# Chunks 0 and 1 of the first mixture: plain float32 out projection, and chunk 1's attention in a fixed order

## The chip, the cores and the metric

The kernel runs on one core of one Trainium2 chip. The metric is the device time of one execution in microseconds; the profile's span, from the first to the last instruction, is shown beside it. Engines are named TensorE (PE in the rows, its weight loads PEld), VectorE (DVE), ScalarE (ACT), GpSimd (POOL) and SyncE (SP, which issues nearly all DMAs here).

## The reference

Three layers follow one another. All arrays are float32; two batches, 8 heads, 768 positions, head width 40, so 1536 tokens of width 320; 1536 hidden columns.

```python
# attention (an mLSTM), for each position t
m_new = max(f_gate + m, i_gate)
C = exp(f_gate + m - m_new) * C + exp(i_gate - m_new) * outer(v, k)
n = exp(f_gate + m - m_new) * n + exp(i_gate - m_new) * k
y[t] = sigmoid(o_gate) * (C @ q) / max(abs(n . q), 1)
# first layer, on all tokens
x = (sigmoid(x @ w_gate) * (x @ w_val)) @ w_out
# second layer, with its own weights
xn = x / sqrt(mean(x * x) + 1e-6) * rms_g
g = xn @ w_gate
out = (g * sigmoid(g) * (xn @ w_val)) @ w_out
```

## The kernel before, in words

**Tiles and steps.** The positions are cut into 6 chunks of 128; a chunk holds both batches, so 256 tokens (`T`), of which batch `b` is one half. The hidden columns are cut into 12 blocks `f` of 128. The first layer is a list of 72 steps (chunk, block): `moe` (line 741) makes 16 gate and value matmuls of 256 columns (line 747) into a PSUM bank `g`; ScalarE takes the sigmoid (749), VectorE the product with the value half (750). `moe_out` (776) multiplies the result `h` with the out weights and accumulates both halves over all 12 blocks in two PSUM banks `o`. The second layer has 36 steps over pairs of chunks (`moe2`, `moe2_out`).

**Split operands.** TensorE works in a reduced float32 format (F32R). An operand is held as a high part and a low part, the difference to the original, and a product is three matmuls. For `h` ScalarE copies the high part (752) and GpSimd subtracts (753, by `sub`, line 194); `moe_out` then has three matmuls a half, six a step (785). Weights are prepared block by block: `load_w` brings a block as packed 64-bit words (960 KB); `conv_w` (138) with `conv_1` and `conv_2` turns the words into float32, two passes on ScalarE (161, 172) and two on VectorE (184, 191); `split_w` (202) makes high parts (copies by ScalarE, 198) and low parts (194, GpSimd or VectorE by the tables `G1`, `O1`) of the gate, value and out weights.

**Attention.** The part of a chunk for one batch: scores (`a_s`, line 357, plain float32), their product with the decay (`a_p`, 366), the inter part from the carried state (`a_inter`, 403 and 405), the weighted sum (`a_pv`, 426), the state update (`a_u`, 435 to 444), and an end (`a_h`, 455 to 464; `a_h0` for chunk 0) that finishes `x`; `a_x` transposes `x` and splits it into `xT` (522 and 194), which the steps of that chunk read.

**Order.** `ORDER` lists the chunk of each of the first 24 steps. Everything else hangs on step numbers: `at(t, ...)` puts a piece of attention, a load or a conversion of weights ahead of step t, and the loop at line 827 issues the events of a step, the step, and the out matmuls of the step `SKEW` = 2 before. A scheduler then chooses the order on each engine; the code up to line 715 (chunk 0's attention, blocks 0 and 1) is pinned by `pin` (716) in the order in which it is written, and what follows is issued behind it.

```python
ORDER = '000000111100001100111111'
C1S = (-4, -2)
```

Of the kernel before, what the change touches and what calls it, by code (L numbers as in the profile page):

```python
# [30 lines left out]
SKEW = 2  # L31
WARM = 5
# [7 lines left out]
ORDER = '000000111100001100111111'  # L40
# [8 lines left out]
PINNED = ('EngineType.PE', 'EngineType.DVE', 'EngineType.Activation', 'EngineType.Pool')  # L49
# [17 lines left out]
def mlstm_moe_kernel(ctx, tc, gate_if, gate_s, qk, qg, tok, w1, w2, rms_g, cst, out):  # L67
# [55 lines left out]
    def load_tok(c, b):  # L123
        t = tok_t[c, b] = p2.tile([128, 8 * 122], F32, tag="tok", name="tok").rearrange("p (h e) -> p h e", h=8)
        nc.sync.dma_start(out=t, in_=tok[c, b])
        if c:
            g = qg_t[c, b] = p1.tile([120, 3, L], F32, tag="qg", name="qg")
            nc.sync.dma_start(out=g, in_=qg[c, b])

    wg_t, wo_t, wraw, wc, conv = {}, {}, {}, {}, {}  # L130

# [69 lines left out]

    def split_w(f, go=0, oo=0, both=True, eng=None):
# [3 lines left out]
        w = wo_t[f] = wp.tile([128, 2, DM], F32R, tag=f"wo{f}", name="wo")  # L206
        eng = eng or nc.scalar
        copy(eng, t[:, :, 0:2, :], g)
        copy(eng, t[0:64, 0, 2, :], r[0:64])
        copy(eng, t[64:128, 1, 2, :], r[64:128])  # L210
        copy(eng, w[:, 0, :], o)

        def low():
            sub(nc.vector, t[64:128, 0, 2, :], r[0:64], t[0:64, 0, 2, :])
            sub(nc.gpsimd, t[0:64, 1, 2, :], r[64:128], t[64:128, 1, 2, :])

        if go:
# [314 lines left out]
    def a_x(c, b):  # L532
# [65 lines left out]
    at(16, lambda: nc.gpsimd.tensor_scalar(out=rmsg, in0=rmsg, scalar1=2.0 ** -16, scalar2=None, op0=ALU.mult))  # L598
# [41 lines left out]
    load_w(w1, 1)  # L640
    p = nc.gpsimd
# [21 lines left out]
    a_p(0, 1)  # L663
    gates_r2()
# [61 lines left out]
    after = ExitStack()  # L726
    for k in pin(first).values():
        after.enter_context(tc.issue_after(k))
    nc.sync.dma_start(out=selg, in_=cst[0:U, CW:CW + 120])
    nc.sync.dma_start(out=selc, in_=cst[0:U, CW + 120:])  # L730
    nc.sync.dma_start(out=rmsg, in_=rms_g)
    gates_r5()
# [4 lines left out]
    load_qk(1, 0)  # L737
    load_tok(1, 0)


    def moe(c, f):
# [7 lines left out]
        nc.scalar.activation(out=sg, in_=g[:, 0, :], func=AF.Sigmoid, scale=2.0 ** -8)  # L749
        nc.vector.tensor_tensor(out=sg, in0=sg, in1=g[:, 1, :], op=ALU.mult)  # L750
# [25 lines left out]
    def moe_out(c, f):  # L776
        h = hst.pop((1, c, f))
        w = wo_t_used[1, f]
        for b in range(B):
# [3 lines left out]
            n = slice(b * L, (b + 1) * L)  # L783
            for i, (hs, ws) in enumerate(((0, 0), (0, 1), (1, 0))):
# [42 lines left out]
    for i in range(min(ev), len(seq) + SKEW):  # L827
# [10 lines left out]
        while 0 <= i and done < len(seq) and done <= i - (SKEW if seq[done][0] == 1 else 1):  # L838
# [87 lines left out]
```

## Time and profile before

| | us |
|---|---|
| median of 3 runs (518.36 to 520.56) | 518.44 |
| the profiled execution | 518.81 |
| its span | 517.0 |
| TensorE busy | 490.7 |
| VectorE busy | 306.6 |
| GpSimd busy | 238.5 |
| ScalarE busy | 228.9 |

The mean granted TensorE clock over the span is 0.969 of full speed. Busy time is the union of an engine's instructions. Matmuls are pipelined, so a busy TensorE is not one at its peak; what a matmul costs in a row of equal ones is read from start to start. A plain float32 matmul stands in the trace as two records, a reduced one as one. In a row, `out<-in` are the program's names, `xN` is a count, and the idle time behind a row names what ended it.

### The profile page before, as it was taken

To read this page: it belongs to the slowest core of one execution; us is meant where nothing else is said; L and a number is where in the kernel's file an instruction comes from. 1 tells how busy PE (TensorE), PEld (TensorE's weight loads), DVE (VectorE), ACT (ScalarE), POOL (GpSimd) and SP (SyncE) were. 2 spreads that over 40 slices of the span, in tenths; PEclk is the share of its full clock that TensorE was granted. 3 is DMA by queue.
4 is the path that set the end of the run, shared out by engine and by line. 5 is a ranking of instruction groups with operands and counts; after the bars stand their busy time and mean duration, and the time that the engine had idled before them with its cause. 6 is when DMAs were issued, how large, how long until landed. Compare 5 with 4: busy or idle time off the path is not lost.

```text
span 517.0 us, 8591 instructions
## 1 busy us (share of the span) xinstructions
PE 490.7 (95%) x3324; PEld 445.8 (86%) x3324; DVE 306.6 (59%) x551; ACT 228.9 (44%) x507; POOL 238.5 (46%) x267
## 2 busy tenths in 40 slices
PE   8896958999999999999999978999999999999997
PEld 5676847999999999999999867888888888888886
DVE  6869989853285785967878996723243223432223
ACT  3655757523354443445468756522243222431222
POOL 2758884653355545644337995621212221122220
PEclk9977966999999999999999999999999999999999
DMA  7667656220031140302354323100010000100001
GB/s 243 185 231 234 226 196 222 90 81 30 12 121 37 44 150 11 81 16 77 112 199 166 136 77 105 48 0 2 0 53 0 1 0 2 45 7 1 0 1 51
DMA packets 12558, 42.60 MB, mean 82 GB/s; under 512 B 1590, under 2 KB 4870, under 8 KB 12518
## 3 DMA queue, kind: packets, MB, share of 16 engines
q1 hardware_dynamic: 12278, 41.84, 24.3%
q8 instruction: 26, 0.43, 0.3%
q10 hardware_dynamic: 240, 0.22, 0.2%
q14 instruction: 14, 0.11, 0.1%
HBM read 40.05 MB, written 2.00 MB: 81 GB/s over the span
## 4 chain that ended last, share of the span: by engine, by line
PE 72%; DVE 12%; POOL 5%; DMA 4%; ACT 4%; issue 3%; POOLq 0%; ACTq 0%; SPq 0%
PE g L747 13%; PE g L761 13%; PE a L761 13%; PE o L810 12%; PE o L785 8%; DMA wraw<-in_w_dram 4%; PE o L747 3%; DVE wg L194 2%; DVE wc L184 2%; POOL wg L194 2%; DVE wc L191 1%; POOL wo L194 1%; PE a L357 1%; ACT wg L198 1%; POOL h L194 1%
## 5 line engine op out<-in xcount | busy, mean ns | idle before, releaser
L747 PE MATMUL g<-xT,wg 128*128 128x256 f32 x912 | 130.6, 295 | 1.8 <-DVE sig L750 1.3
L747 PEld LDWEIGHTS g<-xT,wg 128*128 128x128 f32 x912 | 121.2, 200 | 4.1 <-DVE sig L750 1.5
L194 POOL TENSOR_TENSOR ft<-p,fb 128x512 fp32r<-128x512 f32 x35 | 45.2, 1292 | 131.0 <-ACT fb L770 131.0
L194 POOL TENSOR_TENSOR h<-sig,h 128x256 fp32r<-128x256 f32 x72 | 64.7, 900 | 77.3 <-ACT h L752 76.3
L785 PE MATMUL o<-wo,h 128*128 128x320 f32 x432 | 79.7, 317 | 12.2 <-POOL h L194 10.4
L764 DVE TENSOR_TENSOR p<-p,g 128x512 f32<-128x512 f32 x36 | 24.5, 687 | 92.1 <-ACT p L763 92.1
L785 PEld LDWEIGHTS o<-wo,h 128*128 128x128 f32 x432 | 65.9, 192 | 15.2 <-POOL h L194 12.5
L810 PE MATMUL o<-wo,fb 128*128 128x320 f32 x288 | 52.9, 310 | 0.0
L763 ACT ACTIVATE p<-g 128x512 f32<-128x512 f32 x36 | 21.3, 596 | 67.6 <-PE g L761 64.6
L761 PE MATMUL g<-xT,wg 128*128 128x512 f32 x180 | 50.8, 394 | 0.1
L770 ACT ACTIVATE fb<-p 128x512 fp32r<-128x512 f32 (+1 forms) x37 | 22.8, 620 | 61.2 <-DVE p L769 55.0
L761 PE MATMUL a<-xT,wg 128*128 128x512 f32 x180 | 47.7, 390 | 0.0
L810 PEld LDWEIGHTS o<-wo,fb 128*128 128x128 f32 x288 | 45.6, 188 | 2.0
L752 ACT ACTIVATE h<-sig 128x256 fp32r<-128x256 f32 x72 | 29.7, 414 | 39.5 <-DVE sig L750 38.8
L761 PEld LDWEIGHTS a<-xT,wg 128*128 128x128 f32 x180 | 33.6, 188 | 6.8
L769 DVE TENSOR_TENSOR p<-p,a 128x512 f32<-128x512 f32 (+1 forms) x37 | 24.6, 672 | 23.1 <-PE a L761 23.1
L761 PEld LDWEIGHTS g<-xT,wg 128*128 128x128 f32 x180 | 32.6, 188 | 5.6 <-ACT xT L480 0.4
L750 DVE TENSOR_TENSOR sig<-sig,g 128x256 f32<-128x256 f32 x57 | 23.5, 414 | 21.2 <-ACT sig L749 19.8
L747 PE MATMUL o<-xT,wg 128*128 128x256 f32 x240 | 34.9, 290 | 0.0
L749 ACT ACTIVATE sig<-g 128x256 f32<-128x256 f32 x57 | 21.5, 377 | 29.4 <-PE g L747 21.9
L194 POOL TENSOR_TENSOR wg<-wc,wg 128x256 fp32r<-128x256 f32 (+1 forms) x34 | 28.9, 862 | 9.4 <-ACT wg L198 7.4
L747 PEld LDWEIGHTS o<-xT,wg 128*128 128x128 f32 x240 | 31.2, 191 | 0.5 <-issue 0.5
(249 smaller groups left out, 842.2 us busy)
## 6 DMA issues: line engine op xcount, KB each, us to landing
wraw<-in_w_dram SPq DMA_DIRECT2D x24, 960.0 KB
tok<-in_tok_dram SPq DMA_DIRECT2D x12, 488.0 KB
fb<-fd SPq DMA_DIRECT2D x16, 256.0 KB
raw<-in_qk_dram SPq DMA_DIRECT2D x24, 160.0 KB
out_dram<-xn SPq DMA_DIRECT2D x12, 160.0 KB
qg<-in_qg_dram SPq DMA_DIRECT2D x10, 180.0 KB
rmsg<-in_rms_g_dram SPq DMA_DIRECT2D x1, 160.0 KB
cs<-in_cst_dram ACTq DMA_DIRECT2D x1, 136.5 KB
```

Of the source, the lines that this page charges most:

```text
L194: eng.tensor_tensor(out=out, in0=a, in1=b, op=ALU.subtract)
L747: nc.tensor.matmul(out=g[:, m, :], lhsT=w[:, m, ws, :], rhs=x[xs // 3][:, xs % 3, :], start=(i == 0), stop=(i == 7))
L749: nc.scalar.activation(out=sg, in_=g[:, 0, :], func=AF.Sigmoid, scale=2.0 ** -8)
L750: nc.vector.tensor_tensor(out=sg, in0=sg, in1=g[:, 1, :], op=ALU.mult)
L752: nc.scalar.activation(out=h[:, 0, :], in_=sg, func=AF.Copy)
L761: nc.tensor.matmul(out=g[m], lhsT=w[:, m, ws, :], rhs=x[xs // 3][:, xs % 3, :], start=(i == 0), stop=(i == 7))
L763: nc.scalar.activation(out=sg, in_=g[0], func=AF.Sigmoid, scale=2.0 ** -8)
L764: nc.vector.tensor_tensor(out=sg, in0=sg, in1=g[0], op=ALU.mult)
L769: nc.vector.tensor_tensor(out=sg[:, n], in0=sg[:, n], in1=g[1][:, n], op=ALU.mult)
L770: nc.scalar.activation(out=h[0][:, n], in_=sg[:, n], func=AF.Copy)
L785: nc.tensor.matmul(out=o, lhsT=h[:, hs, n], rhs=w[:, ws, :], start=(f == 0 and i == 0), stop=(f == NF - 1 and i == 2))
L810: nc.tensor.matmul(out=o, lhsT=h[hs][:, n], rhs=w[:, ws, :], start=(f == 0 and i == 0), stop=(f == NF - 1 and i == 2))
```

## The change

**Out projection of chunks 0 and 1.** `NAT` = 2 names the chunks. For them VectorE's product is written to `h` as plain float32, with no copy and no subtraction, and `moe_out` has one float32 matmul a half. The out weights of all 12 blocks stay whole at first: `conv_2` writes them straight to their place (`keep`), in two pieces. `split_o` splits them afterwards, with an event at step 23 + f, each block into the place of the block before it (`new_wo`). The out matmuls of these chunks follow one step after their step, not two.

**Order.** The first 24 steps are now blocks 0 to 3 of chunk 0, blocks 0 to 3 of chunk 1, then blocks 4 to 11 for chunk 0 and 1 in turn. Chunk 1's attention is no longer put by events: its scores for batch 0 are issued before step 0, the rest by `early(i)` behind steps 0 to 3, with blocks 1 to 3's conversion, and the order of all engines, SP now too, is pinned up to step 7 (`NPIN` = 8). The small loads, chunk 1's loads and the gate transposes (`gates_r5a` to `c`) stand in that part as well; ten of the thirteen filler matmuls just before step 0 go, in part for chunk 1's scores.

```diff
-ORDER = '000000111100001100111111'
+ORDER = '000011110101010101010101'
-PINNED = ('EngineType.PE', 'EngineType.DVE', 'EngineType.Activation', 'EngineType.Pool')
+PINNED = ('EngineType.SP', 'EngineType.PE', 'EngineType.DVE', 'EngineType.Activation', 'EngineType.Pool')
@@ conv_2
-        nc.vector.scalar_tensor_tensor(out=c, in0=hi, scalar=-0x80000000, in1=c, op0=ALU.bitwise_and, op1=ALU.bitwise_or)
+        cut = ((c, 0, WC),)
+        if f in keep:
+            w = wo_t[f] = wp.tile([128, 2, DM], F32, tag=f"wo{f}", name="wf")[:, 0, :]
+            cut = (c[:, 0:640], 0, 640), (w.bitcast(I32), 640, WC)
+        for o, a, b in cut:
+            nc.vector.scalar_tensor_tensor(out=o, in0=hi[:, a:b], scalar=-0x80000000, in1=c[:, a:b], op0=ALU.bitwise_and, op1=ALU.bitwise_or)
@@ split_w
-        copy(eng, w[:, 0, :], o)
+        if f not in keep:
+            copy(eng, w[:, 0, :], o)
...
+    def split_o(f, oo):
+
+        o = wo_t[f]
+        w = wo_t[f] = new_wo(f)
+        copy(nc.scalar, w[:, 0, :], o)
         sub(nc.vector if oo else nc.gpsimd, w[:, 1, :], o, w[:, 0, :])
@@ the events
+        at(NF * NAT + f - 1, split_o, f, O1[f])
-        if f >= 2:
+        if f >= 6:
             at(t - LW, load_w, w1, f)
-        if f >= 2:
+        if f >= 4:
+            at(t - CV, keep.add, f)
             at(t - CV, conv_w, f, "wc", L1[f], True, SG1[f])
@@ before step 0
     idle = bank("o3")
-    busy(idle, *[512] * 6)
-    xT_dup(xT[1, 0], 0, x[:, 0], "o2")
-    a_h0(1)
     busy(idle, *[512] * 3)
+    xT_dup(xT[1, 0], 0, x[:, 0], "o2", False)()
+    conv_w(1, "wc", 1, False)
+    a_s(1, 0, "aa")
     xT_dup(xT[1, 0], 1, x[:, 1], idle)
-    pend.append(4)
@@ moe
+        if c < NAT:
+            h = hst[1, c, f] = hp.tile([128, 2, T], F32R, tag="h", name="h")[:, 0, :].bitcast(F32)
+            nc.vector.tensor_tensor(out=h, in0=sg, in1=g[:, 1, :], op=ALU.mult)
+            return
@@ moe_out
+            if c < NAT:
+                nc.tensor.matmul(out=o, lhsT=h[:, n], rhs=w, start=(f == 0), stop=(f == NF - 1))
+                continue
@@ the loop over the steps
+    def early(i):
+
+        if i == 0:
+            split_w(1, 1)
+            a_s(1, 1, ("o2", "o3"))
+            for qd in range(4):
+                a_k(1, qd)
+            a_p(1, 0)
+            a_p(1, 1)
+            conv_w(2)
+        elif i == 1:
+            a_inter(1, 0)
+            load_qg(1, 1)
+            load_w(w1, 4)
+            split_w(2, 1)
...
+            a_pv(1, 0)
+            a_pv(1, 1)
+            a_u(1, 0)
+            conv_w(3)
+            load_w(w1, 5)
+        elif i == 2:
+            a_h(1, 0)
+            split_w(3, 1)
+            a_inter(1, 1, "o2")
+            a_pv(1, 2, "o3")
+            a_pv(1, 3, "o3")
+            a_u(1, 1, "a")
+            a_x(1, 0, "a")
+            a_h(1, 1)
+        elif i == 3:
+            a_x(1, 1, "o2")
...
+        if i == NPIN:
+            for k in pin(first).values():
+                after.enter_context(tc.issue_after(k))
```

How the instructions now stand is shown at two places. The first is VectorE's queue before step 0, at the ends of chunk 0's attention (`r` and `x`) and the low parts of its transposes (`xT`). Before:

```order
L476 TENSOR_TENSOR x<-x,a 128x320
L477 TENSOR_TENSOR x<-x,r 128x320
L159 TENSOR_SCALAR wraw<-wraw 128x960
L194 TENSOR_TENSOR xT<-o_355,xT 128x3x128
L473 TENSOR_SCALAR r<-o_320 128x8
L474 SCALAR_TENSOR_TENSOR r<-o_320,r 128x8
L475 RECIPROCAL r<-r 128x8
L476 TENSOR_TENSOR x<-x,o_320 128x320
L477 TENSOR_TENSOR x<-x,r 128x320
L194 TENSOR_TENSOR xT<-o_348,xT 128x3x128
L194 TENSOR_TENSOR wg<-wc,wg 64x128
```

With the change:

```order
L511 TENSOR_TENSOR x<-x,a 128x320
L512 TENSOR_TENSOR x<-x,r 128x320
L508 TENSOR_SCALAR r<-o_334 128x8
L509 SCALAR_TENSOR_TENSOR r<-o_334,r 128x8
L510 RECIPROCAL r<-r 128x8
L511 TENSOR_TENSOR x<-x,o_334 128x320
L512 TENSOR_TENSOR x<-x,r 128x320
L205 TENSOR_TENSOR xT<-o_387,xT 128x3x128
L176 TENSOR_SCALAR wc<-wraw 128x960
L205 TENSOR_TENSOR xT<-o_383,xT 128x3x128
L205 TENSOR_TENSOR wg<-wc,wg 64x128
```

The five operations that finish the second half of `x` moved ahead of the first low part, and one pass of block 1's conversion moved from ahead of that low part to behind it.

The second place is TensorE's queue at the end of chunk 1's attention: the transposes of its halves (lines 518 and 520, with the change 553 and 555), the out matmuls and the next steps. Before, from the second weighted sum to steps 6 and 7:

```order
L426 MATMUL a<-tok,p 128x42
L435 MATMUL a<-tok,kk 120x126 x2
L435 MATMUL a<-tok,kk 80x84
L785 MATMUL o_645<-wo,h 128x320 x2
L785 MATMUL o_649<-wo,h 128x320 x2
L785 MATMUL o_645<-wo,h 128x320
L785 MATMUL o_649<-wo,h 128x320
L518 MATMUL a<-cs,x 128x128 x2
L520 MATMUL a<-cs,x 64x128 x2
L357 MATMUL a<-raw 128x128 x4
L747 MATMUL g<-xT,wg 128x256 x32
```

With the change, from the end of the first half's attention to step 4:

```order
L553 MATMUL a<-cs,x 128x128 x2
L555 MATMUL a<-cs,x 64x128 x2
L828 MATMUL o_559<-wf,h 128x320
L828 MATMUL o_561<-wf,h 128x320
L786 MATMUL g<-xT,wg 128x256 x16
L553 MATMUL o_670<-cs,x 128x128 x2
L555 MATMUL o_670<-cs,x 64x128 x2
L828 MATMUL o_559<-wf,h 128x320
L828 MATMUL o_561<-wf,h 128x320
L786 MATMUL g<-xT,wg 128x256 x16
L828 MATMUL o_559<-wf,h 128x320
L828 MATMUL o_561<-wf,h 128x320
```

The second transposes moved from ahead of step 6 to ahead of step 4, with steps 3 and 4 pinned behind them, and an out product is one matmul for each half where it was three.

## Rows read from the trace of the kernel before

**Rows 1.** The windows query: busy us of each engine (instructions), granted clock, DMA share, GB/s.

```profile
28.80:99.20 70.40, 56.70 (x356) 51.56 (x356) 62.28 (x83) 45.07 (x89) 50.73 (x55) 0.79 0.60 203
70.00:80.00 10.00, 4.57 (x18) 3.06 (x17) 8.73 (x13) 6.61 (x13) 8.78 (x12) 0.50 0.56 190
99.20:146.80 47.60, 47.60 (x381) 45.66 (x381) 22.59 (x50) 17.16 (x45) 20.40 (x29) 1.00 0.14 41
146.80:290.00 143.20, 143.07 (x1252) 139.15 (x1251) 109.25 (x230) 77.00 (x188) 77.33 (x90) 1.00 0.28 95
```

**Rows 2.** The same for line 747 alone, TensorE's gate and value matmuls.

```profile
28.80:99.20 70.40, 28.04 (x161) 25.91 (x162) 0.79 0.60 203
99.20:146.80 47.60, 30.70 (x224) 28.26 (x225) 1.00 0.14 41
```

**Rows 3.** The same for line 785 alone, the out matmuls.

```profile
99.20:146.80 47.60, 14.74 (x85) 12.58 (x84) 1.00 0.14 41
```

**Rows 4.** TensorE's timeline: start us, us, line, count, [idle before <- releaser].

```profile
26.05 0.44 PE L518 MATMUL o<-cs,x 128*128 128x128 f32 x2 [1.92 <-DVE x L477]
...
77.99 0.69 PE L518 MATMUL a<-cs,x 128*128 128x128 f32 x2 [4.22 <-DVE x L464]
...
81.31 6.07 PE L747 MATMUL g<-xT,wg 128*128 128x256 f32 x32
```

**Rows 5.** The chain of waits in order of time: start us, us, what, count.

```profile
6.60 1.50 PE a L357 x16
...
99.33 1.92 PE g L747 x16
...
116.76 1.71 PE a L426 x16
...
200.83 1.75 PE o L785 x12
```

**Rows 6.** TensorE's timeline around line 403, attention's inter part.

```profile
59.96 0.80 PE L403 MATMUL a<-cm,qg 120*128 120x126 f32 x6
60.55 0.54 PE L785 MATMUL o<-wo,h 128*128 128x320 f32 x2
```

**Rows 7.** Groups by form, 0 to 130 us: busy us, mean ns, idle before.

```profile
L191 DVE SCALAR_TENSOR_TENSOR wc<-wraw,wc 128x960 int32<-128x960 int32 x12 | 15.4, 1280 | 0.2
L184 DVE SCALAR_TENSOR_TENSOR wc<-wraw,wc 128x960 int32<-128x960 int32 x12 | 15.2, 1264 | 3.8 <-ACT wc L172 3.7
L194 POOL TENSOR_TENSOR h<-sig,h 128x256 fp32r<-128x256 f32 x18 | 15.0, 837 | 14.8 <-ACT h L752 14.7
...
L194 DVE TENSOR_TENSOR wg<-wc,wg 64x128 fp32r<-64x128 f32 x12 | 9.4, 780 | 2.3 <-ACT wg L198 1.9
...
L194 POOL TENSOR_TENSOR wo<-wc,wo 128x320 fp32r<-128x320 f32 x8 | 8.8, 1101 | 0.5
...
L319 DVE TENSOR_TENSOR_SCAN ft<-fb,ident 128x512 f32<-128x512 f32 x6 | 7.6, 1288 | 0.0
L750 DVE TENSOR_TENSOR sig<-sig,g 128x256 f32<-128x256 f32 x18 | 7.4, 415 | 7.4 <-ACT sig L749 6.1 <-POOL cm L444 1.2
...
L366 DVE TENSOR_TENSOR p<-a,ft 128x512 f32<-128x512 f32 x6 | 4.0, 686 | 1.4 <-PE a L357 0.9 <-ACT ft L335 0.5
...
L194 DVE TENSOR_TENSOR wg<-wc,wg 128x512 fp32r<-128x512 f32 x4 | 3.5, 880 | 0.1
...
L442 DVE SCALAR_TENSOR_TENSOR C<-C,gb,a 120x126 f32<-120x126 f32 x8 | 2.5, 338 | 1.0 <-PE a L435 1.0
...
L403 PEld LDWEIGHTS a<-cm,qg 120*128 120x128 f32 x16 | 2.2, 191 | 0.1
L194 DVE TENSOR_TENSOR xT<-a,xT 128x384 fp32r<-128x384 f32 x4 | 2.1, 549 | 3.1 <-ACT xT L522 3.1
```

**Rows 8.** VectorE's timeline: the first and the next line after chunk 1's first attention end.

```profile
52.21 0.51 DVE L455 TENSOR_TENSOR hs<-a,hs 128x336 f32<-128x336 f32 x1
...
55.38 1.69 DVE L184 SCALAR_TENSOR_TENSOR wc<-wraw,wc 128x960 int32<-128x960 int32 x1
```

More of the change, by code (lines that the diff above doesn't have):

```diff
@@ L31 @@
 SKEW = 2
+NAT = 2
+NPIN = 8
 WARM = 5
@@ L121, in load_qk, with load_qg, load_tok @@
             nc.sync.dma_start(out=t[64 * j:64 * j + D], in_=qk[c, 2 * b + j, 0:D])
-    def load_tok(c, b):
+    def load_qg(c, b):
+        g = qg_t[c, b] = p1.tile([120, 3, L], F32, tag="qg", name="qg")
+        nc.sync.dma_start(out=g, in_=qg[c, b])
+    def load_tok(c, b, q=True):
         t = tok_t[c, b] = p2.tile([128, 8 * 122], F32, tag="tok", name="tok").rearrange("p (h e) -> p h e", h=8)
         nc.sync.dma_start(out=t, in_=tok[c, b])
-        if c:
-            g = qg_t[c, b] = p1.tile([120, 3, L], F32, tag="qg", name="qg")
-            nc.sync.dma_start(out=g, in_=qg[c, b])
+        if c and q:
+            load_qg(c, b)
     wg_t, wo_t, wraw, wc, conv = {}, {}, {}, {}, {}
+    keep = set()
     more = []
@@ L200, in copy, with new_wo @@
             eng.tensor_copy(out=out, in_=in_)
+    old = set()
+    def new_wo(f):
+        if f == 0 and not old:
+            old.add(0)
+            return p2.tile([128, 2 * 4 * L], F32R, tag="qkr", name="wo")[:, 0:2 * DM].rearrange("p (s n) -> p s n", s=2)
+        return wp.tile([128, 2, DM], F32R, tag=f"wo{(f + NF - 1) % NF}", name="wo")
     def split_w(f, go=0, oo=0, both=True, eng=None):
@@ L210, in split_w @@
         copy(eng, t[64:128, 1, 2, :], r[64:128])
-        copy(eng, w[:, 0, :], o)
+        if f not in keep:
+            copy(eng, w[:, 0, :], o)
         def low():
             sub(nc.vector, t[64:128, 0, 2, :], r[0:64], t[0:64, 0, 2, :])
-            sub(nc.gpsimd, t[0:64, 1, 2, :], r[64:128], t[64:128, 1, 2, :])
+        sub(nc.gpsimd, t[0:64, 1, 2, :], r[64:128], t[64:128, 1, 2, :])
         if go:
@@ L223, in split_w @@
             low()
+        if f not in keep:
+            sub(nc.vector if oo else nc.gpsimd, w[:, 1, :], o, w[:, 0, :])
+        keep.discard(f)
+        return low
+    def split_o(f, oo):
+        o = wo_t[f]
+        w = wo_t[f] = new_wo(f)
+        copy(nc.scalar, w[:, 0, :], o)
         sub(nc.vector if oo else nc.gpsimd, w[:, 1, :], o, w[:, 0, :])
-        return low
     gp = stk.enter_context(tc.tile_pool(name="gp", bufs=1))
@@ L568, in mlstm_moe_kernel @@
     pos = {k: i for i, k in enumerate(seq)}
-    for c in range(1, NC):
+    for c in range(2, NC):
         for b in range(B):
-            s0 = C1S[b] if c == 1 else C2S[b] if c == 2 else 12 * (c - 1) + 6 * b + S0
+            s0 = C2S[b] if c == 2 else 12 * (c - 1) + 6 * b + S0
             qa, qb = 2 * b, 2 * b + 1
-            if c > 1 or b > 0:
+            if True:
                 at(s0 - 4, load_qk, c, b)
                 at(s0 - 3, load_tok, c, b)
-            d = EV1 if c == 1 else EV2
+            d = EV2
             assert s0 + d[12] <= pos[1, c, 0]
@@ L640, in mlstm_moe_kernel @@
     load_w(w1, 1)
+    nc.sync.dma_start(out=selg, in_=cst[0:U, CW:CW + 120])
+    nc.sync.dma_start(out=selc, in_=cst[0:U, CW + 120:])
+    nc.sync.dma_start(out=rmsg, in_=rms_g)
     p = nc.gpsimd
@@ L689, in mlstm_moe_kernel @@
     a_pv(0, 1, "a")
+    keep.update((0, 1, 2, 3))
     conv_w(0, "wc", 2, False, 0, True)
     conv_1(0)
+    gates_r5a()
     conv_2(0)
@@ L724, in pin @@
         return chain
[L726 to L732, printed above, removed]
     stk.close()
@@ L826, in mlstm_moe_kernel @@
     done = 0
-    for i in range(min(ev), len(seq) + SKEW):
+    after = ExitStack()
+    def early(i):
[12 more added lines that the diff above has]
+            split_w(2, 1)
+            a_p(1, 2, p2.tile([128, 4, L], F32, tag="ft", name="p"))
+            a_p(1, 3, p2.tile([128, 4, L], F32, tag="ft", name="p"))
+            a_o(1, 0)
+            a_o(1, 1)
+            a_pv(1, 0)
[14 more added lines that the diff above has]
+            a_x(1, 1, "o2")
+    assert min(ev) >= 0, min(ev)
+    for i in range(len(seq) + SKEW):
+        if i == NPIN:
+            for k in pin(first).values():
+                after.enter_context(tc.issue_after(k))
         if i == 24 + SKEW:
@@ L837, in mlstm_moe_kernel @@
             (moe if layer == 1 else moe2)(c, f)
-        while 0 <= i and done < len(seq) and done <= i - (SKEW if seq[done][0] == 1 else 1):
+            if i < NPIN:
+                early(i)
+        while 0 <= i and done < len(seq) and done <= i - (SKEW if seq[done][0] == 1 and seq[done][1] >= NAT else 1):
             layer, c, f = seq[done]
```

34 lines of the change are left out of this document (20 added, 14 removed).

## The prediction, made before the run

> **What bounds the kernel now.** I read the windows first, then the counts of one line in the same windows, then TensorE's timeline, then prices by form. The windows [rows 1] divide the run at step 0 (28.8 us) and at step 24 (146.8 us), the first that belongs to neither chunk 0 nor chunk 1. From 99.2 us on, TensorE is busy 47.60 of 47.60 us and then 143.07 of 143.20, at the full clock: there the time is TensorE's own work, and only less work on it would help. Between 28.8 and 99.2 us it is busy 56.70 of 70.40 us, and the granted clock averages 0.79; with the two levels 2.4 and 1.2 GHz, a mean of 0.79 means that 0.42 of the stretch, 29.6 us, ran at 1.2; between 70 and 80 us all of it did, with TensorE busy 4.57 of 10 us. VectorE is busy 62.28 us of these 70.4, GpSimd 50.73. The counts say how little got done: the gate and value matmuls come 16 to a step, 161 of them (10 steps) in those 70.4 us, 224 (14 steps) in the next 47.6 [rows 2]. The timeline names the waits: 1.92 us before the transposes of chunk 0's second half, 4.22 us before those of chunk 1's second half, both for the VectorE product that finishes x; only then come steps 6 and 7 [rows 4]. So the early stretch is set by VectorE's queue, with GpSimd beside it, and the clock falls in the same stretch in which TensorE waits.
>
> **What a step costs on TensorE.** At full clock 16 matmuls of 256 columns take 1.92 us, and 12 reduced-precision matmuls of 320 columns 1.75, so 0.146 each [rows 5]; a step's six out matmuls cost 0.88. The change has two plain float32 matmuls in their place. No row shows one with 320 columns. The nearest is line 403, plain float32: three matmuls stand as six records, four of 126 and two of 84 columns, and the next line starts 0.59 us after the first [rows 6]: 0.88 ns a column, two records a matmul. For 320 columns that is 0.281 us a record, and four records, 1.12 us a step: 0.24 more than now. Lower end: a record no dearer than a reduced-precision matmul, 4 x 0.146 = 0.58. Upper end: each record also waits for its whole weight load, 0.191 us [rows 7], which line 403 hides: 4 x 0.472 = 1.89. I take 1.12, from the one plain float32 row whose cost follows its columns; over 24 steps it adds 5.8 us.
>
> A rule speaks against this part. The Trainium skill, "FP8 and Floating Point Precision", section "TensorE Precision Notes", counts four passes through the array for true float32, where three reduced-precision products are replaced. Four passes at the 0.146 us of the 320-column row would be 0.58 a matmul, 1.17 a step, so 7.0 us over 24 steps instead of 5.8: the price rises, but the sum hardly moves.
>
> **What leaves and what moves.** For chunks 0 and 1, VectorE's product at line 750 writes h itself. ScalarE's copy of h and GpSimd's subtraction go (24 each; the subtraction 0.84 us [rows 7]), and so do the copy and subtraction of the out weights before step 24 (the latter 1.10 us on GpSimd), which come back in twelve calls of split_o from step 23 on in the source; the order has the first already around step 8. From step 24 on they lie beside a TensorE that is always busy, with GpSimd at 77 of 143 us [rows 1], so I cost them at nothing; without that cover they would be 8 x 1.10 us on GpSimd. conv_2's last operation in two pieces costs VectorE one more start, within 0.1 us each. Order needs only weights 0 to 3 for steps 0 to 7, then one more every second step, where before weights 0 to 5 were wanted by step 5 and 6 to 9 in steps 10 to 13. On SP the loads of chunk 2's tokens and gate rows move behind the weights 2 to 6; nothing before step 8 reads them.
>
> **Step 0.** Now x of chunk 0's second half is finished before the first half's low part, and the gate transposes, four fillers and the 1.92 us wait [rows 4] no longer stand between it and step 0; chunk 1's first score matmuls (1.50 us) fill part of that wait. Step 0 moves from 28.8 to about 26.8.
>
> **To step 4.** From there VectorE's queue runs, in the order of the change, without a gap that I can find, to chunk 1's last transposed low part. At the row means [rows 7]: four conversions of weights 1 to 4 at 1.26 + 1.28 (10.2), four h at 0.41 (1.6), three 512-wide subtractions at 0.88 (2.6), four small ones at 0.78 (3.1), four products with the decay at 0.69 (2.8), the inter part's scaling twice at some 0.55 (1.1), the state update twice at 3 x 0.34 (2.0), two attention ends of 3.17 (52.21 to 55.38) [rows 8], and two low parts at 0.55 (1.1): 30.8 us. Started at 27.0, this ends at 57.8. Step 4 needs it after its fifth matmul: eleven more take 1.3, step 3's out 1.1, and step 5 starts at 60.2. TensorE's queue is pinned there: the transposes of chunk 1 stand ahead of the out matmuls and of steps 3 and 4, and everything behind waits with them.
>
> **To step 24.** 19 steps of 1.92 (36.5) and 19 outs of 1.12 (21.3). Attention: of the 47.6 us before step 24, 14 steps take 26.9 and the 85 out matmuls 12.4 [rows 3], which leaves 8.3 for it; chunk 2 had 4.4 more before 99.2 (scores 1.50, inter 0.59, weighted sum 1.71 [rows 5, 6], update about as the inter part, 0.6). That is 12.7, and step 24 would come at 60.2 + 70.5 = 130.7. Two losses are added. The clock: the walk has TensorE idle for 3 us or so before each transpose of chunk 1, as it now is in the 10 us at 0.50 [rows 1], so steps 3 to 5 run partly at 1.2 GHz; most of that hides behind VectorE, and I take 3 us. Steps 8 to 18: VectorE has five conversions (12.7), five small subtractions (3.9), ten h (4.1), three wide ones (2.6) and chunk 2's attention (per half two scans of 1.29, two products of 0.69, an end of 3.17, and some 2.2 more: 9.3, so 18.7), in all 42 us beside TensorE's 10 steps of 3.04 and that attention's 10.2 (per half scores 1.5, inter 0.6, weighted sum 1.7, update 0.6 and some 0.7 for transposes), 41: equal loads in queues that each keep their order, and I take 2.5 us as lost. Step 24 at 136.2 instead of 146.8 is 10.6 gained; behind it one out (1.12) is left over where before two were (1.76), 0.6 more. The later rows of the order are the same but for a few places, so the rest is carried along: 518.81 - 11.2 = 507.6 against the profiled execution, which lies 0.37 above the median of the three runs: **507.2 us**.
>
> **Rivals.** First, all goes well: POOL leaves VectorE alone (its 64-row subtraction has a mean of 0.78, so the queue to step 4 could be 2.4 us shorter), the clock holds and nothing is lost in steps 8 to 18: 2.4 + 3 + 2.5 = 7.9 less, 499.3. For it: in those 70 us GpSimd loses a third of its early work. Against: the idle stretches before the two transposes stay. Beside this stands the Trainium skill, "SBUF — State Buffer", section "Who interferes with whom", by which VectorE and GpSimd lock a shared port pair for a whole instruction; no row of mine separates that from other waits.
> Second, VectorE becomes the bound in steps 8 to 18 and loses 7.5 us instead of 2.5: 512.2.
> Third, no change: the pinned chain is longer than its prices, because conversions wait for ScalarE's two passes or for a load. Step 5 at 71 instead of 60 gives everything back: 518. Against: 11 us on a queue of 31 is more than any wait of the trace.
> Fourth, slower: float32 weight loads are not hidden when a 320-column record has to be streamed. Place: the out matmuls of steps 0 to 23; price: 24 x (1.89 - 1.12) = 18.5, so 525.7; it decides from 0.40 us a record on (0.281 + 11.2/96). Against: line 403 hides them.
> That the change does not do what it says can be put aside: the order shows two out matmuls a step and the pinned sequence.
>
> **How the numbers follow.** Forecast 0.50; all well 0.20; VectorE bound 0.16; no change 0.08; slower 0.06. A measurement of this kernel tells about 0.5%, 2.6 us, from no change: faster is 0.86. The range reaches to the first two rivals and the tails around the second: 499 to 515, leaving out the last two and a little below.
>
> **What would show it.** Right: step 0 near 27, step 5 between 58 and 64, step 24 between 130 and 140 us; out records near 0.28 us apart; the stretch after step 24 as long as before. Wrong: out records above 0.4 apart; idle TensorE between steps 8 and 24; GpSimd or ScalarE named as releaser in steps 24 to 36.

## The result and the profile after

| | us |
|---|---|
| the changed kernel, median of 4 runs (503.63 to 505.98) | 504.76 |
| the kernel before, beside it on the same chip, median of 4 runs (518.36 to 520.56) | 518.91 |
| ratio, 95% interval | 0.9723 (0.9690 to 0.9756) |
| the profiled execution; its span | 505.04; 503.2 |
| the span before | 517.0 |

The change gains 2.8%; the forecast was 507.2 us, with a range from 499 to 515. Now and then an execution of these kernels is some 3% longer at a lower granted clock; the medians and ratios here and below leave those out. The span falls by 13.8 us, of which 13.2 are there at step 24: it comes at 133.6 us instead of 146.8. Behind it 369.6 us follow, before 370.2.

The windows of the changed kernel, columns as in [rows 1], cut at steps 0, 5, 9, 16 and 24:

```profile
26.30:54.40 28.10, 25.28 (x180) 21.80 (x181) 25.40 (x52) 14.31 (x28) 8.85 (x15) 0.94 0.45 154
54.40:67.70 13.30, 13.30 (x99) 11.76 (x97) 8.66 (x12) 10.71 (x19) 6.04 (x7) 1.00 0.84 270
67.70:103.10 35.40, 31.03 (x199) 26.87 (x197) 28.71 (x42) 15.37 (x29) 20.74 (x25) 0.90 0.55 200
103.10:133.60 30.50, 29.44 (x207) 25.89 (x205) 18.27 (x36) 12.33 (x30) 8.49 (x10) 1.00 0.11 37
133.60:276.80 143.20, 143.03 (x1238) 138.21 (x1237) 109.89 (x233) 78.41 (x193) 76.11 (x91) 1.00 0.30 97
```

To step 5, VectorE is busy 25.40 of 28.10 us, and GpSimd, which had 50.73 of 70.40 [rows 1], is busy 8.85. From 54.4 to 67.7 TensorE is never idle. From 67.7 on it is again (4.4 us to step 16, 1.1 more to step 24), and the clock falls. The long stretch behind step 24 is as it was [rows 1].

TensorE's timeline shows the price of the plain out (line 786 is the gate and value matmuls, 828 the out), and the chain of work and waits that ended last gives it directly:

```profile
54.40 2.32 PE L786 MATMUL g<-xT,wg 128*128 128x256 f32 x16
56.56 1.24 PE L828 MATMUL o<-wf,h 128*128 128x320 f32 x4
57.39 2.32 PE L786 MATMUL g<-xT,wg 128*128 128x256 f32 x16
```
```profile
115.32 1.08 PE o L828 x4
```

From step to step 3.00 us pass, of which 1.92 are the sixteen matmuls: four records of 320 columns cost 1.08, 0.27 each or 0.84 ns a column, two cycles of the 2.4 GHz clock.

What TensorE waits for between 63.4 and 133.6 us (us in total, times, longest), then the two long waits in its timeline and the out matmuls that follow, and the windows behind each wait:

```profile
PE o L828 <- DVE h L791: 2.9, 2, 2.3
PE a L438 <- DVE p L401: 2.0, 1, 2.0
```
```profile
72.00 1.13 PE L438 MATMUL a<-cm,qg 120*128 120x126 f32 x4 [2.04 <-DVE p L401]
72.92 2.34 PE L828 MATMUL o<-wf,h 128*128 128x320 f32 x4
...
96.08 2.50 PE L828 MATMUL o<-wf,h 128*128 128x320 f32 x4 [2.33 <-DVE h L791]
```
```profile
72.10:75.50 3.40, 3.40 (x11) 2.61 (x12) 3.37 (x5) 1.83 (x5) 3.33 (x4) 0.50 0.00 0
96.00:99.40 3.40, 3.32 (x9) 2.54 (x10) 3.37 (x8) 2.53 (x5) 0.52 (x1) 0.50 0.34 86
```

Each is followed by 3.4 us at 1.2 GHz (the windows, granted clock 0.50), in which four out records take 2.34 and 2.50 us instead of 1.24. So each wait costs its length and then up to 1.7 us more. A third such stretch, 44.8 to 48.2 us, follows a wait of 1.7 us for x, before step 5.

### The profile page after: what moved, and what is told of

Read it like the earlier page. It is cut to its first block, busy times and chain, and to the rows that moved or that the text cites. A ratio compares the mean times of both kernels' runs of the same rounds, so it can differ in the third digit from the quotient of the medians.

```text
span 503.2 us, 8423 instructions
## 1 busy us (share of the span) xinstructions
PE 485.2 (96%) x3264; PEld 434.8 (86%) x3266; DVE 303.1 (60%) x564; ACT 222.5 (44%) x485; POOL 210.0 (42%) x238
## 4 chain that ended last, share of the span: by engine, by line
PE 65%; DVE 5%; DMA 4%; POOL 3%; issue 2%; ACT 1%; POOLq 0%; ACTq 0%
PE g L804 13%; PE a L804 13%; PE o L856 12%; PE g L786 11%; PE o L831 6%; PE o L786 4%; DMA wraw<-in_w_dram 4%; PE o L828 2%; POOL h L205 1%; POOL wg L205 1%; DVE wg L205 1%; PE a L392 1%; PE a L457 1%; PE a L438 1%; PE a L470 1%
## 5 line engine op out<-in xcount | busy, mean ns | idle before, releaser
L786 PEld LDWEIGHTS g<-xT,wg 128*128 128x128 f32 x912 | 118.2, 193 | 7.2 <-issue 1.7
L205 POOL TENSOR_TENSOR h<-sig,h 128x256 fp32r<-128x256 f32 x48 | 44.9, 938 | 57.2 <-ACT h L795 56.0
L831 PE MATMUL o<-wo,h 128*128 128x320 f32 x288 | 52.0, 313 | 3.9 <-POOL h L205 3.8
L813 ACT ACTIVATE fb<-p 128x512 fp32r<-128x512 f32 (+1 forms) x37 | 22.8, 620 | 60.7 <-DVE p L812 54.5
L806 ACT ACTIVATE p<-g 128x512 f32<-128x512 f32 x36 | 21.3, 596 | 62.9 <-PE g L804 59.8
L831 PEld LDWEIGHTS o<-wo,h 128*128 128x128 f32 x288 | 43.2, 189 | 6.2 <-POOL h L205 5.1
L804 PEld LDWEIGHTS g<-xT,wg 128*128 128x128 f32 x180 | 32.5, 188 | 5.5 <-ACT xT L515 0.4
L828 PE MATMUL o<-wf,h 128*128 128x320 f32 x96 | 34.1, 481 | 2.9 <-DVE h L791 2.9
L788 ACT ACTIVATE sig<-g 128x256 f32<-128x256 f32 x57 | 21.5, 377 | 26.8 <-PE g L786 23.5
L205 POOL TENSOR_TENSOR wg<-wc,wg 128x256 fp32r<-128x256 f32 (+1 forms) x30 | 22.8, 771 | 24.2 <-ACT wg L209 22.4
L167 ACT ACTIVATE wraw<-wraw 128x960 f32<-128x960 f32 x23 | 25.2, 1097 | 14.1 <-DMA wraw<-in_w_dram 13.9
L856 PE MATMUL o<-wo,ft 128*128 128x320 f32 x144 | 31.4, 309 | 0.0
## 6 DMA issues: line engine op xcount, KB each, us to landing
cs<-in_cst_dram ACTq DMA_DIRECT2D x1, 136.5 KB
```

Source lines behind the costliest of these rows:

```text
L167: nc.scalar.activation(out=hi.bitcast(F32), in_=hi.bitcast(F32), func=AF.Copy, scale=2.0 ** -111)
L205: eng.tensor_tensor(out=out, in0=a, in1=b, op=ALU.subtract)
L786: nc.tensor.matmul(out=g[:, m, :], lhsT=w[:, m, ws, :], rhs=x[xs // 3][:, xs % 3, :], start=(i == 0), stop=(i == 7))
L804: nc.tensor.matmul(out=g[m], lhsT=w[:, m, ws, :], rhs=x[xs // 3][:, xs % 3, :], start=(i == 0), stop=(i == 7))
L806: nc.scalar.activation(out=sg, in_=g[0], func=AF.Sigmoid, scale=2.0 ** -8)
L813: nc.scalar.activation(out=h[0][:, n], in_=sg[:, n], func=AF.Copy)
```

## The experiments

Each kernel ran beside the kernel before, whose median was 518.9 to 520.5 us from one group of runs to the next; its ratio is to the runs beside it, so kernels are compared by their ratios rather than their medians. The steps and the span are those of one profiled execution each. Starts of steps 5 and 24 are those of the first record of line 786 (or the line that answers to it) in TensorE's timeline.

| kernel | median us | ratio (95%) | step 5 | step 24 | span |
|---|---|---|---|---|---|
| before | 518.9 | 1 | 59.8 | 146.8 | 517.0 |
| the change | 504.8 | 0.9723 (0.9690 to 0.9756) | 54.4 | 133.6 | 503.2 |
| e1, order with the split out | 507.7 | 0.9770 (0.9741 to 0.9800) | 59.3 | 133.6 | 505.0 |
| e2, plain out in the old order | 518.1 | 0.9971 (0.9957 to 0.9984) | 58.6 | 148.6 | 517.2 |
| e4, GpSimd's subtractions of h back | 510.0 | 0.9815 (0.9789 to 0.9841) | 54.8 | 138.3 | 507.4 |
| e15, ScalarE work back, early | 507.5 | 0.9755 (0.9721 to 0.9789) | 57.7 | 136.5 | 505.7 |
| e3, second buffer | 505.1 | 0.9716 (0.9689 to 0.9744) | 54.2 | 134.5 | 504.1 |
| e5, out two steps behind | 500.3 | 0.9621 (0.9583 to 0.9659) | 53.9 | 128.4 | 497.9 |
| e6, splits late | 503.5 | 0.9677 (0.9641 to 0.9713) | 53.7 | 130.9 | 500.7 |
| e9, e5 and e6 | 501.9 | 0.9652 (0.9616 to 0.9688) | 54.5 | 128.1 | 501.9 |
| e8, more out columns | 513.9 | 0.9875 (0.9842 to 0.9907) | 55.6 | 142.7 | 512.3 |

In the kernel before and in e2, step 5 is still chunk 0's; their step 6 came at 81.3 and 77.2. Behind step 7 each kernel's order is set anew by the scheduler, so differences of less than about 1 us between two kernels are not read as effects. The profiled execution of e1, e4 and e6 is the fastest of its kernel, by 0.7 to 1.0 us against the median, and that of e9 the slowest, by 1.7.

**e1 and e2: the order and the plain out apart.** The change has three parts: the order, the plain out, and an out one step behind its gate matmuls instead of two. The distance hangs on `NAT` too, so it goes back to two steps in e1 and becomes one in e2. e1 keeps the new order and takes the plain out away:

```diff
-NAT = 2
+NAT = 0
-    keep.update((0, 1, 2, 3))
-        at(NF * NAT + f - 1, split_o, f, O1[f])
-            at(t - CV, keep.add, f)
```

> The new order of steps 0 to 23 and of chunk 1's attention, but with h and the out weights split as before: three reduced-precision out matmuls a token block, h's copy and GpSimd subtraction 24 times, all twelve out weights split before they are used. Theory (the order gains, and the plain out makes room on GpSimd for it): an out costs 0.88 us instead of 1.12, but GpSimd has 24 x 0.84 + 12 x 1.10 = 33 us more before step 24, and VectorE's operations beside it are longer, so step 5 starts near 60 instead of 54.4, step 24 near 139 instead of 133.6, and the time is 508 to 511 us. Rival A (the order does it all, plain float32 only costs): step 5 at 54, step 24 near 129, 499 to 501 us. Rival B (the plain out does it all): step 5 after 62, at least 515 us.

e2 is the kernel before, its order untouched, with `NAT = 2` and the change's code for it:

```diff
+        if c < NAT:
+            h = hst[1, c, f] = hp.tile([128, 2, T], F32R, tag="h", name="h")[:, 0, :].bitcast(F32)
+            nc.vector.tensor_tensor(out=h, in0=sg, in1=g[:, 1, :], op=ALU.mult)
+            return
...
+            if c < NAT:
+                nc.tensor.matmul(out=o, lhsT=h[:, n], rhs=w, start=(f == 0), stop=(f == NF - 1))
+                continue
```

> The kernel before with the plain float32 out of chunks 0 and 1 alone, its order of steps and its attention of chunk 1 as they were. Theory (the order gains most): the waits before the two transposes of x stay, six steps of chunk 0 are still done before chunk 1's x is there; freed GpSimd shortens VectorE's queue by 2 to 3 us, the dearer out matmuls cost 5.8 us only where TensorE is never idle (some 8 of the 24 steps, 2 us): 516 to 519 us. Rival B (the plain out does it all): at most 508 us. Rival C (TensorE's price is paid in full): 523 us or more.

e1 has step 5 at 59.3, as expected, and a time just under the theory's 508 to 511 us, but step 24 at 133.6, where the changed kernel has it too: of the 13.2 us at step 24, the order with the split out two steps behind brings all, and by the ratios 2.3 of the 2.8%. Plain out and shorter distance together gain 4.9 us to step 5 and give 4.9 back to step 24 (79.2 us instead of 74.3). They are not the same thing: e5, below, has the plain out at e1's distance, and beside e1 it has step 5 5.4 us and step 24 5.2 us sooner, with ratios of 0.9621 and 0.9770 whose intervals lie apart. So the plain out is worth 1.5% in the new order, and the distance hides 1.0% of it in the changed kernel. e2 came out as the theory had it, 0.3% faster; whether the plain out would gain more in the old order at two steps was not tried. TensorE's wait for chunk 1's x stands in it as before [rows 4]:

```profile
PE a L545 <- DVE x L491: 4.2, 1, 4.2
```

Why e1 is later at step 5 stands in VectorE's waits, first in e1 from 26.7 to 59.3 us, then in the changed kernel to 54.4:

```profile
DVE wg L205 <- ACT wg L209: 1.8, 3, 1.1
DVE sig L787 <- ACT sig L782: 1.7, 1, 1.7
DVE xT L205 <- ACT xT L554: 0.9, 1, 0.9
DVE wc L190 <- ACT wc L178: 0.9, 2, 0.4
```
```profile
DVE h L791 <- ACT sig L788: 1.9, 1, 1.9
DVE xT L205 <- ACT xT L557: 0.2, 1, 0.2
```

The windows are e1's, then the changed kernel's:

```profile
26.70:59.30 32.60, 25.66 (x180) 23.41 (x180) 26.74 (x47) 17.00 (x35) 15.56 (x24) 0.84 0.41 138
```
```profile
26.70:54.40 27.70, 24.88 (x179) 21.40 (x178) 25.00 (x52) 14.31 (x28) 8.77 (x14) 0.94 0.44 150
```

VectorE waits for ScalarE 5.3 us instead of 2.1, and is busy 26.74 us instead of 25.00: together the 4.9. In e1 ScalarE has four copies of h (416 ns) and four of out weights (470 ns) more in that stretch. Two causes offer themselves, ScalarE's queue and GpSimd beside VectorE; the next kernels put one of them back each.

**e4: GpSimd's subtractions of h put back** (those of the out weights stay away).

```diff
+            sub(nc.gpsimd, t[:, 1, :], h, sg)
```

> The changed kernel with one idle GpSimd subtraction of 128x256 more in each step of chunks 0 and 1 (h minus sg into h's unused half, read by nobody), TensorE's, ScalarE's and VectorE's work unchanged. Theory (GpSimd's work beside VectorE lengthens VectorE's operations, which set steps 0 to 4 and much of 8 to 18): 24 subtractions of 0.84 us take from VectorE about a quarter of their 20 us, step 5 starts 1.5 to 3 us later, the time is 508 to 511 us. Rival (what GpSimd does beside it is of no account; the early queue was priced too dear for another reason): step 5 within 0.5 us of 54.4, 504 to 506 us.

The time is as the theory said, the place is not. GpSimd is busy 13.79 us from 26.7 us to step 5 instead of 8.77 (15.56 in e1), and step 5 comes only 0.4 us later. The other 4.3 us are lost from there to step 24, where TensorE waits at the out alone:

```profile
PE o L830 <- DVE h L792: 8.1, 5, 2.9
```

Five waits for h, 8.1 us, instead of two, 2.9, among waits of 5.3 us in all.

**e12 and e15: ScalarE's work put back**, in all of chunks 0 and 1, and for weights 0 to 3 alone (with the `f < 4`).

```diff
+            if f < 4:
+                copy(nc.scalar, t[:, 1, :], h)
...
+        elif f < 4:
+            copy(eng, wf_t[f][:, 1, :], wo_t[f])
```

> The changed kernel with the ScalarE work of the split put back and nothing else: a copy of h (0.42 us) in each step of chunks 0 and 1 and a copy of each out weight (0.47 us) where its split stood, into unused halves that nobody reads. Theory (in steps 0 to 4 VectorE's queue waits for ScalarE's, so the change gained its 5 us there by what it took from ScalarE, and by what it took from GpSimd only in the second place): VectorE waits for ScalarE 2 to 3.5 us more before step 5, which starts at 56.5 to 58, and the time is 506.5 to 509 us. Rival (ScalarE has room for it): step 5 within 0.7 us of 54.4, 504 to 505.5 us.

> The changed kernel with the ScalarE work of the split put back for weights 0 to 3 alone, that is in steps 0 to 7: eight copies of h (0.42 us) and the copies of three out weights on ScalarE (0.47 us; that of weight 0 is on GpSimd), into unused halves that nobody reads. Theory (VectorE's queue to step 4 waits for ScalarE's as soon as these copies stand in it, and the other 5 us or so of the 7.6 that all the copies cost arise after step 8): step 5 starts 1.5 to 3.5 us later than 54.4, step 24 as much later than 133.6, 506 to 508.5 us. Rival A (early, ScalarE has room for them, all of the cost arises after step 8): step 5 within 0.7 us, 504 to 505.5 us. Rival B (all of it arises early): 510 us or more.

e12 took 512.3 us (ratio 0.9837, 0.9795 to 0.9880): the sign was right, the cost larger than expected, and where its later part arises was not followed up. e15 shows the early part, step 5 at 57.7 and 507.5 us, both inside the theory's bounds. VectorE's timeline has the new waits where ScalarE's copies stand ahead of what VectorE needs (its waits for ScalarE come to 5.3 us to step 5, as in e1):

```profile
31.08 1.23 DVE L206 TENSOR_TENSOR wg<-wc,wg 128x512 fp32r<-128x512 f32 x2 [1.05 <-ACT wg L210]
...
37.83 1.23 DVE L206 TENSOR_TENSOR wg<-wc,wg 128x512 fp32r<-128x512 f32 x2 [0.58 <-ACT wg L210]
```

So the early gain of the plain out, 4.9 us, is mostly ScalarE's (3.3 in e15) and little GpSimd's alone (0.4 in e4). The other 1.2 us show in neither; VectorE is busy 1.6 us longer in e1 than in e15. Both loads together were not put back.

**e3: SP's queue.** In the changed kernel SP issues chunk 2's second tokens at 61.09 and the gate queries behind them at 77.56, since their one buffer is free only after the last records of line 438, at 77.18; weights 8 follow at 78.00. e3 gives them a buffer:

```diff
+        if (c, b) == (2, 1):
+            g = p2.tile([128, 2 * 4 * L], F32R, tag="qkr", name="qg")[0:120, 0:3 * L].bitcast(F32).rearrange("p (g t) -> p g t", g=3)
```

> The changed kernel with a buffer of its own for the gate queries of chunk 2's second half, so that SP does not hold their load, and the loads of weights 8 and 9 and of the decay rows behind it, until the inter matmuls of the first half have run. Theory (in steps 8 to 18 SP's blocked queue is the cause of half the loss): the issue of weights 8 moves from 78 to about 62 us, VectorE's idle 5.7 us between 78.6 and 84.3 goes, step 24 comes 3 to 5 us sooner, 500 to 502 us. Rival (VectorE's own load sets these steps, the late loads only fill its gaps): step 24 within 1 us, 504 to 506 us.

SP is free, as its timeline shows (the gate queries at 61.30, weights 8 at 65.74), and the time is the same: the rival holds.

```profile
61.30 0.43 SPq L131 DMA_DIRECT2D qg<-in_qg_dram  x1
65.74 0.33 SPq L146 DMA_DIRECT2D wraw<-in_w_dram  x1
```
```profile
PE o L832 <- DVE h L795: 3.4, 3, 2.5
PE a L442 <- DVE p L405: 2.5, 1, 2.5
```

TensorE's waits for VectorE (second fence) are there as before, 5.9 us against 5.3.

**e5: the out two steps behind.** The change had also set the out of chunks 0 and 1 one step behind its gate matmuls, where it was two.

```diff
-done <= i - (SKEW if seq[done][0] == 1 and seq[done][1] >= NAT else 1)
+done <= i - (SKEW if seq[done][0] == 1 else 1)
```

> The changed kernel with the out matmuls of chunks 0 and 1 two steps behind their gate matmuls instead of one. Theory (TensorE waits for h because the plain out comes only one step behind it, while VectorE has other work ahead of h in its queue): the 2.9 us of waits of line 828 go, and the half-speed spell after 96 us with them, step 24 comes 3 to 5 us sooner, 500 to 502 us. Rival (VectorE is behind anyway, and the wait moves to the next thing that TensorE wants from it): step 24 within 1.5 us, 503.5 to 506 us.

500.3 us, as the theory had it, and the best of all kernels here. The waits for h at the out are gone; the first row is all that TensorE still waits for VectorE's h, at the gate matmuls of a later step. The windows are the changed kernel's, then e5's:

```profile
PE g L786 <- DVE h L791: 2.6, 3, 1.3
PE a L553 <- DVE C L477: 0.4, 1, 0.4
```
```profile
63.40:133.60 70.20, 64.77 (x439) 56.49 (x437) 50.88 (x82) 31.86 (x67) 31.64 (x36) 0.95 0.38 133
```
```profile
63.40:133.60 70.20, 67.21 (x475) 57.85 (x474) 52.53 (x86) 33.56 (x72) 35.53 (x38) 1.00 0.43 143
```

TensorE is idle for 3.0 instead of 5.4 us and the clock never falls. From step 5 to 24 e5 takes 74.5 us instead of 79.2, and as long as e1 with its cheaper out. Two more pairs below differ in the distance alone: e3 and e11 take 80.3 and 76.5 us there, e6 and e9 77.2 and 73.6. So two steps are worth 3.6 to 4.7 us there.

**e6 and e9: the splits of the out weights.** Each split is queued behind what its engines were given before it:

```diff
+        with ExitStack() as late:
+            for e in (nc.scalar, eng):
+                late.enter_context(tc.issue_after(last[e.engine]))
             copy(nc.scalar, w[:, 0, :], o)
```

> The changed kernel with each of the twelve splits of the out weights held back, on ScalarE and on GpSimd or VectorE, behind the work of the step before which the source names it (23 to 34), as the prediction had costed them; in the changed kernel the scheduler has eight of them between 64 and 104 us. Theory (GpSimd's and VectorE's time is worth something in steps 8 to 18, and nothing after step 24): VectorE has 1.9 us and GpSimd some 8 us less before step 24, which comes 1.5 to 3 us sooner, the stretch after it stays as it was, 502 to 503.5 us. Rival A (they lie in gaps there): 504 to 506 us. Rival B (after step 24 they hold up the out matmuls of chunk 2): 507 us or more.

> Both at once: out matmuls of chunks 0 and 1 two steps behind, and the splits of the out weights held back to steps 23 to 34. Theory: the two gains add, 498 to 501 us. Rival (both touch the same waits, or TensorE's own work is left as the bound): no better than the better of the two alone, within 1 us.

e6 has step 24 2.7 us sooner; by the ratios, whose intervals overlap, a gain is likely but not certain. TensorE waits no less than in the changed kernel:

```profile
PE o L833 <- DVE h L796: 5.7, 5, 1.7
```

But none of the five waits is longer than 1.7 us, and the granted clock is 1.00 from step 5 to 24: what e6 saves are the half-speed stretches. In e9 nothing adds: step 24 stands at 128.1, e5's 128.4, and behind it e9 takes 373.8 us where e5 takes 369.5. Of these 4.3 us 1.0 are two waits of TensorE in chunk 3's attention; the profiled execution of e9 is its slowest, that of e5 its fastest, and by the medians e9 loses 1.6. Where that goes was not followed up.

**e8: more out columns.**

```diff
+                nc.tensor.matmul(out=o_ps[c, b][:, DM:512], lhsT=h[:, n], rhs=w[:, 0:512 - DM], start=False, stop=(f == NF - 1))
```

> The changed kernel with 192 more columns, read by nobody, in a second plain float32 matmul behind each out matmul of chunks 0 and 1, into the unused part of the same bank: 24 steps x 2 matmuls x 2 records x 192 columns at 0.88 ns is 0.68 us a step, 16.2 us in all, 12.8 from step 5 on. Theory (from step 5 to 24 TensorE's work is the bound but for some 5 us): a step of 5 to 8 takes 3.68 us instead of 3.00, step 24 comes 9 to 13 us later, 514 to 518 us. Rival (VectorE is the bound from step 8 to 18): only some nine of the steps pay, step 24 comes 4 to 7 us later, 509 to 512 us.

```profile
59.19 2.21 PE L786 MATMUL g<-xT,wg 128*128 128x256 f32 x16
61.24 0.70 PE L828 MATMUL o<-wf,h 128*128 128x320 f32 x2
61.78 0.49 PE L829 MATMUL o<-wf,h 128*128 128x192 f32 x2
...
62.83 2.21 PE L786 MATMUL g<-xT,wg 128*128 128x256 f32 x16
```

A step takes 3.64 us (59.19 to 62.83), so 768 record columns cost 0.64, 0.83 ns each. Step 24 comes 9.1 us later, the theory's lower end. From step 5 on 19 x 0.64 = 12.2 are added and 7.9 show: the rest fills TensorE's idle time, and the clock does not fall: 1.00 over 63.4 to 133.6 us, where the changed kernel has 0.95.

**e11 and e14: is there more in e5?** e11 is e5 with e3's buffer; e14 is e5 with the plain out for weights 0 to 3 alone (`if c < NAT and f < NPL`, NPL = 4).

> The kernel with the out matmuls two steps behind (500.3 us) and also the second buffer for the gate queries, so that SP does not hold the loads behind it. Theory (the loads matter once TensorE no longer waits for h): 1 to 2.5 us more, 498 to 499.5 us. Rival (as alone, the late loads only fill VectorE's gaps): 499.7 to 501.5 us.

> The kernel with the out matmuls two steps behind (500.3 us), but plain float32 only for out weights 0 to 3 of chunks 0 and 1 (eight steps), the other eight weights and their h split as before the change. Theory (from step 8 on TensorE's work is the bound when nothing makes it wait): 16 steps x 0.24 = 3.8 us of TensorE's work go, GpSimd gets 16 x 0.84 + 8 x 1.10 us more, and about half of the gain is left: 497.5 to 499.5 us. Rival (the load on GpSimd, ScalarE and VectorE is worth more than TensorE's time there, as the added GpSimd work showed): 501 us or more.

Neither: 501.9 us (0.9640, 0.9602 to 0.9679) and 502.4 (0.9639, 0.9594 to 0.9683), both the rival's. In e14, 3.2 us less work on TensorE (16 steps x 0.20) does not shorten the time; which of the other engines takes it back was not looked at.

## Why the prediction held, and where it did not

**The time held, in part by luck: two terms were wrong by more than the forecast's error, and partly cancelled.** Predicted gain 11.2 us, measured 13.8 (span). Step 5 came 5.8 us sooner than forecast, and of that 4.0 were lost again by step 24.

*The price of the plain out: right.* 1.08 us a step against the 1.12 taken. The record of line 403 was the right row. The rule of the Trainium skill ("FP8 and Floating Point Precision", "TensorE Precision Notes"), four passes, agrees: two records of two cycles a column are four cycles a column, where a reduced-precision record takes 1.1 (0.146 us for 320 columns [rows 5]). The estimate by it, 1.17, is 0.09 high. The fourth rival, exposed weight loads, is ruled out by the 0.27 us a record.

*Step 0: right,* 26.3 against 26.8.

*VectorE's queue to step 4: the term that was mis-sized most.* It was priced at 30.8 us at the row means of the kernel before. From 26.7 to the last low part at 52.0 us it took 25.3 (VectorE's timeline of the changed kernel), so step 5 came at 54.4, outside the 58 to 64 given as right.

```profile
26.74 0.28 DVE L205 TENSOR_TENSOR wg<-wc,wg 64x128 fp32r<-64x128 f32 x1
...
51.44 0.55 DVE L205 TENSOR_TENSOR xT<-o,xT 128x384 fp32r<-128x384 f32 x1
```

The means, taken over 0 to 130 us of the old order, held dearer rows than stand in this stretch now. The groups by form of the changed kernel, 26.7 to 54.4 us, have the wide subtraction at 0.69 us instead of 0.88 and the small one at 0.36 instead of 0.78 [rows 7]; the two attention ends, 2.3 and 2.0 us from the first row to the next line's, had been priced at 3.17 [rows 8].

```profile
L205 DVE TENSOR_TENSOR wg<-wc,wg 128x512 fp32r<-128x512 f32 x3 | 2.1, 685 | 0.0
L205 DVE TENSOR_TENSOR wg<-wc,wg 64x128 fp32r<-64x128 f32 x5 | 1.8, 360 | 0.2
```

Little of that is the plain out's doing. In e1, which keeps the split's work, the wide one takes 0.99 us, but the small one 0.47 and the ends 2.5 and 2.0; from the first pass of weights 1 to the last low part its VectorE takes 26.1 us without its waits for ScalarE, the changed kernel 24.9. So the split's work beside it lengthened VectorE's rows by some 1.1 us, and the rest of the 5.5 was too dear for the order alone as well. That e1 has step 5 at 59.3, near the 60.2 of the forecast, is luck: its queue gets there with 3.3 us of waits for ScalarE, where the forecast had a queue without a gap. The first rival named cheaper rows ("POOL leaves VectorE alone"), at 2.4 us. ScalarE's queue, which e15 shows to weigh more than GpSimd's early on, was not priced in the forecast at all.

*Steps 8 to 18: too small a loss.* The forecast took 2.5 us for VectorE and 3 for the clock; from step 5 to 24 the work, 70.5 us less 19 x 0.04 for the cheaper out, is 69.7, and 79.2 passed. Of the 9.5 lost, 5.4 are idle TensorE and 3.4 the two half-speed spells (3.4 us each, half of it lost); 0.7 is left unexplained. So the forecast's own sign of being wrong, idle TensorE between steps 8 and 24, did appear. In size this is near the second rival, which had VectorE lose 7.5 us instead of 2.5. Its reason holds in part: VectorE is not busy all of that time, but where TensorE waits, VectorE is working through rows that stand ahead of p or h in its queue. VectorE waits for ScalarE's sigmoid, that is, for TensorE, 10.9 us from 63.4 to 133.6 us (first row), but only 2.5 of it from 64 to 110 (second row):

```profile
DVE h L791 <- ACT sig L788: 10.9, 5, 2.6
```
```profile
DVE h L791 <- ACT sig L788: 2.5, 1, 2.5
```

What turned VectorE's late h into a loss is that the out was moved from two steps behind to one: e5, with the same instructions, loses 4.7 us less between steps 5 and 24 (79.2 against 74.5). The prediction counted that move as a gain of 0.6 us (one out left over at step 24) and missed that h is then wanted one step sooner. The 0.6 does not show either: behind step 24 the changed kernel takes 369.6 us and the kernel before 370.2, but e5, with two outs left over, 369.5.

*The clock:* it did run at half speed in step 3, from 44.8 to 48.2 us, while VectorE's queue went on without a gap, so the 3 us for steps 3 to 5 were no loss of their own; the spells that cost time came later.

*split_o at nothing:* half right. The order had shown the first ones around step 8, where TensorE is not always busy, and holding them back moves step 24 by 2.7 us in e6. Behind step 24 they are free there, as forecast: e6 takes 369.8 us, the changed kernel 369.6. With the out two steps behind, holding them back gains nothing (e9).

## What to carry to other kernels

Row means hold the neighbours of their own stretch and order: when a change reorders work, price VectorE's queue from the fastest rows of each form as one end and keep the mean as the other. Look for the waits of the queues beside it as well; here ScalarE's weighed more than the lengths of VectorE's rows. An operation that is cheaper in preparation but follows its producer more closely can lose in waits most of what it saved; the distance in steps is a parameter of its own, here worth 4.7 us of the 5.4 that the plain out had gained to step 5. An experiment that takes one part of a change away must be read for what else goes with it, as the distance did in e1. Add a wait's aftermath to its price: in the changed kernel three waits of 1.7 to 2.3 us were each followed by 3.4 us at half clock, while in e6 five waits of up to 1.7 us were not.

## What the hardware showed unexpectedly

VectorE's 64x128 subtraction, all operands in SBUF, takes 0.28 us with GpSimd idle, and once took 2.49 us beside a run of GpSimd operations without a gap. VectorE's timeline of the changed kernel, then GpSimd's:

```profile
93.09 2.49 DVE L205 TENSOR_TENSOR wg<-wc,wg 64x128 fp32r<-64x128 f32 x1
95.60 0.42 DVE L791 TENSOR_TENSOR h<-sig,g 128x256 f32<-128x256 f32 x1
...
113.40 0.28 DVE L205 TENSOR_TENSOR wg<-wc,wg 64x128 fp32r<-64x128 f32 x1
```
```profile
90.80 2.23 POOL L478 TENSOR_TENSOR cm<-C,cs 120x252 f32<-120x252 f32 x1 [2.56 <-DVE C L477]
93.00 0.36 POOL L479 TENSOR_TENSOR cm<-C,cs 80x84 f32<-80x84 f32 x1
93.32 0.75 POOL L415 TENSOR_TENSOR vv<-tok,tg 128x336 f32<-128x336 f32 x1
94.03 1.93 POOL L205 TENSOR_TENSOR wg<-wc,wg 128x256 fp32r<-128x256 f32 x3
```

The one at 93.09 held up h (line 791, behind it) and so the out at 96.08. Line 791 itself, with one input in PSUM, takes 0.41 to 0.42 us on the mean in the kernel before, the changed one, e1 and e4. That agrees with the Trainium skill, "SBUF — State Buffer", "Who interferes with whom": a VectorE instruction with two SBUF inputs contends with a GpSimd instruction that reads SBUF. In the prediction this stood as unproved, and no run here separates it from other causes of a long VectorE row, a DMA's among them. What one such load costs in all, e4 shows: 24 GpSimd subtractions that nobody reads, each with two inputs in SBUF, cost 4.2 us of span.
